# Total decay on ScalarE, a shared power for the norm, centring from PSUM, and a new written-out head order

## The chip, the cores and the metric

The kernel runs on one NeuronCore of a Trainium2 chip. The metric is the device time of one execution in microseconds. The kernel before takes 791.49 us (median of three runs, 790.57 to 791.54).

## What is computed

Inputs are float32 except the weights, which arrive as float64 words. Batch 4, 8 heads, 768 positions, head width 48; model width 384.

```
attention:  f = sigmoid(f_logit)                       # per position and channel
            state = f[t] * state + k[t] (outer) v[t]   # 48 x 48 per head, t = 0..767
            y[t]  = q[t] @ state
norm + mlp: xn = (x - mean) / sqrt(var + 1e-6) * g
            x  = x + relu(xn @ w_ch1) @ w_ch2          # 384 -> 1536 -> 384
token mix:  u  = x + (relu(x^T @ w_tok1) @ w_tok2)^T   # 768 -> 256 -> 768
mlp:        out = u + relu(u @ w_ch1') @ w_ch2'
```

## The kernel before

The attention is cut into 24 units, one for each chunk of 128 positions (six) of each batch (four). A unit's name is its number n, chunk n // 4 of batch n % 4. Its steps have short names, and a name such as `5.lnc` is step `lnc` of unit 5:

- `lf`, `lq`, `lv`: loads of the forget logits, of k and q, and of v, issued by SyncE (SP).
- `clamp` (L280), `log` (two ScalarE instructions, L284 and L285), `scan` (running sum of the logarithms, VectorE, L289), `ek` and `eq` (exponentials, L294 and L298), `km` and `qm` (k and q times these, L301 and L304).
- `tot` (L308, L309): two GpSimd copies of the last column of the sum and of `eq`, into the table `gtot` that a check reads at the end, and into `dec`, the unit's total decay.
- `kp`, `kt`: k transposed by TensorE and copied out; `sc`, `st`: scores and the state's increment; `A0`, `A1`: scores times the triangle (VectorE); `stm`, `ste`, `std`: the new state (`std`, L377, multiplies it by the total decay).
- `y`, `z` (L386, L395): the output in PSUM; `yw` orders two halves; `yc0`, `yc1`, `yt` transpose it back into the PSUM tile `y` (L438).
- `lna` (L444, L447): ScalarE copies `y` to the SBUF tile `x`, summing it; `lnc` (L454): VectorE subtracts the mean and multiplies by g; `tp` (L506), `ah`, `al` (L535, L539): transposed and split into a high and a low part. `lnv` (L457) sums squares, `lnr` (L461, L462) makes the reciprocal root on GpSimd, one unit at a time.

The weights come as 64-bit words. For each of the 24 pieces, `wN.ld` loads it, `wN.a`, `.b`, `.c` (L208, L213, L218) make a float32 of it on VectorE, `.h` is the high part (ScalarE, L230) and `.l` the low part (L231). Pieces w0 to w11 belong to the first matrix, w12 to w23 to the second.

The first MLP works on steps of three units. Steps 0 and 1 are interleaved by halves of the hidden width: `m0.3` is one hidden block of step 0 (nine matmuls, L553), `m0.h3` and `m0.l3` its parts (L568, L572), `m0.o20` nine matmuls of the second matrix for unit 2 (L583), `m0.r01` the scaled addition to x (L650), `m0.d0` the store of the finished x to `x1_d` (L653). `m0.o00`, `m0.o10`, `m0.o20` need w12 to w14, `m0.o01` and its like w15 to w17. The tile `x` has nine buffers, so that `9.lna` needs the buffer that `m0.d0` gives back.

A list of names, ORDER, sets the order of all this work up to the end of step 1 on every engine, as each engine runs its instructions in the order in which they are written. A name in the set POOL goes to GpSimd and not to VectorE. `0.kp+14` puts 14 matmuls on zeros ahead of `0.kp`. Behind the list, units and steps follow by a formula (the steady part, up to some 390 us), then token mixing and the second MLP.

```
def lna: x = xp.tile(..., tag="x") ; activation(out=x, in_=t["y"], func=Copy, accum_out=t["nm"])
def lnc: nc.vector.scalar_tensor_tensor(t["xn"], xs[n], t["nm"][:, 0:1], gln, op0=ALU.add, op1=ALU.mult)
```

Of the kernel before, what the change touches and what calls it, by code (L numbers as in the profile page):

```python
# [31 lines left out]
G_MAX = 40.0  # L32
# [14 lines left out]
    3.clamp 0.km 4.clamp 1.km 1.qm 2.km 3.km 3.qm w12.l 5.clamp 4.km 4.qm w1.l w2.l w0.l 6.clamp 5.qm 5.km w4.l  # L47
    w3.l w5.l 6.qm 6.km w13.l w14.l 7.clamp w17.l w15.l 7.qm 9.clamp w18.l 8.km w6.l 8.qm w11.l w7.l 10.clamp w8.l
    9.qm 9.km 10.qm w19.l w20.l w22.l w21.l w23.l 11.km 11.qm
""".split())  # L50
ORDER = """
    0.lf 0.clamp 1.lf 2.lf 1.clamp 0.log 3.lf 3.clamp 0.scan 0.lq 1.log 0.eq 0.ek 4.lf 0.km 0.kp+14 4.clamp 0.lv
    2.clamp 1.scan 1.lq 0.qm 0.sc 3.log 2.log 0.kt 3.scan 1.ek 2.scan 0.st 0.tot w12.ld 0.A0 0.stm 2.lq 1.lv 0.y+3
# [2 lines left out]
    2.kt w1.a 1.yw w1.b 3.lv 4.ek w2.ld 3.km w0.ld w1.c 0.tp 5.lf 0.ah 1.z 1.yc0 3.qm 1.yc1 2.st w1.h 0.al 2.A0
    2.A1 3.kp 3.kt 4.lq 0.std 2.y 2.stm 4.eq w2.a w12.l 1.yt 1.lna 2.yw 2.tot w3.ld 2.ste 2.z 2.yc0 4.tot 3.sc
    w0.a w2.b 2.yc1 w0.b 1.lnc 4.lv w4.ld 3.st 0.lnv 3.A0 2.yt 3.stm 5.clamp 2.lna 3.A1 3.ste 4.km 3.y+3 3.yw
    5.log 1.tp w2.c 3.z 2.lnc 3.yc0 w0.c 3.yc1 4.qm 6.lf 5.scan w1.l 4.kp+3 2.tp 1.ah 4.kt 4.sc 2.ah w2.h 5.lv
    5.lq 3.yt w5.ld w0.h 1.al 4.st 2.al w2.l 5.ek 3.lna w3.a w17.ld 4.A0 4.A1 m0.1 w13.ld 2.lnv 4.y w4.a w0.l w3.b  # L60
    5.eq 1.lnv 6.clamp w14.ld 6.log 4.stm w3.c 3.lnc m0.2 4.yw w4.b 4.z m0.h1 m0.0 5.qm 4.ste 4.yc0 m0.h2 w4.c
    3.tp 6.lq 5.km 5.kp w4.h w5.a 5.tot 4.yc1 m0.h0 5.sc w16.ld 6.scan w5.b w4.l w3.h m0.l2 w5.c 5.kt 4.yt 1.std
    m0.l0 w5.h 4.lna 5.st 5.A1 6.eq 5.A0 5.stm w3.l w13.a m0.l1 m0.4 5.y w5.l 7.lf 6.qm 6.ek 3.ah w14.a w13.b
    w9.ld 5.ste 5.yw m0.3 m0.h4 6.km w13.c w13.h w14.b w17.a w14.c w17.b 5.z m0.5 m0.l4 5.yc0 5.yc1 w14.h w13.l
    w15.ld m0.h3 w14.l 6.kp 6.sc 6.lv w16.a 6.kt m0.h5 5.yt 7.clamp w17.c m0.l3 3.lnv w15.a w16.b w17.h 5.lna
    w16.c m0.l5 w15.b w15.c m0.o00 m0.o20 4.lnc 7.log m0.o10 6.tot 4.tp w17.l 1.lnr w15.h w16.h 6.st 5.lnc 5.tp
    w16.l w6.ld w18.ld 2.std 4.ah w15.l m0.o01 5.ah m0.o21 3.al 5.std 2.lnr w9.a 7.scan 0.lnr m0.o11 8.lv 7.eq
    5.al 7.ek 4.al m0.r01 w8.ld 6.A0 6.stm m0.r21 8.lf 8.clamp 6.y w18.a m0.r11 m1.2 5.lnv m1.0 7.tot 7.lq m1.h2
    7.km 6.yw w6.a 6.ste 6.A1 7.lv 8.log m1.l2 7.qm m1.1 9.lf 7.kp 8.scan m1.5 4.std 6.z m1.h1 m1.l1 w9.b 4.lnv
    w18.b 7.kt m1.3 m1.h0 8.eq m1.h5 w6.b m1.l0 6.yc0 w9.c w18.c 8.ek m1.h3 w18.h 7.sc 8.lq w11.ld 3.lnr 4.lnr  # L70
    9.clamp w18.l m1.l5 9.log 6.yc1 w6.c w9.h 8.tot m1.l3 m1.4 7.st m1.o10 9.scan w8.a 6.yt 7.A0 w9.l 3.std m1.h4
    w11.a m1.o20 7.y m1.l4 w6.h w11.b 9.eq 8.km w6.l 8.qm 11.lf 5.lnr m1.o11 6.lna 9.ek w7.ld w10.ld w11.c 7.A1
    7.stm 7.yw 7.ste w11.h w22.ld w7.a w7.b w7.c w8.b w11.l m1.r11 m1.o21 m1.r21 w7.h 9.tot 11.clamp 10.lv w10.a
    8.kp w10.b w10.c 8.kt 10.lf 11.log 8.sc 7.z m1.o00 6.std w7.l w10.h 7.yc0 8.st 11.scan w10.l 8.A0 m0.7 m1.o01
    w19.ld w8.c m1.r01 w22.a w21.ld 8.y 10.clamp w22.b m0.h7 m0.10 m0.6 w22.c w8.h 9.lq 8.yw 8.A1 m0.l7 7.yc1 9.lv
    8.stm 7.yt w19.a m0.h10 m0.h6 11.ek m0.l6 11.eq 6.lnc w20.ld 8.z 8.yc0 m0.l10 8.ste 10.log m1.11 w8.l m0.9
    m1.h11 9.qm 9.km 9.kp 9.sc 10.scan 9.kt m0.8 10.ek 7.lna m0.h9 8.yc1 w19.b w20.a m1.l11 w20.b 9.st w19.c 10.eq
    m0.h8 w19.h m0.11 8.yt 10.lq 11.lv 9.A0 m0.h11 10.qm m0.l8 m1.7 8.lna m0.l9 w19.l 9.stm 9.ste w22.h 10.km 9.y
    10.kp s2.ld 9.A1 m1.8 m0.l11 9.yw m1.9 w20.c m1.h7 10.kt w20.h 8.std s0.ld s1.ld w20.l 9.z 6.tp w21.a w22.l
    8.lnc w21.b m1.h9 9.yc0 m1.l7 w23.ld 10.sc 7.std 6.lnv 10.tot m1.l9 w23.a w21.c s1.a 6.ah 6.al w23.b w23.c  # L80
    9.yc1 7.lnc 6.lnr w21.h 8.tp m1.6 8.lnv m1.h6 8.ah m1.h8 w21.l m1.10 w23.h 9.std 10.st m1.l8 10.A0 w23.l
    10.stm m1.l6 7.tp 10.ste s0.a 7.lnv 9.yt m1.h10 9.lna m0.o22 m1.l10 s0.b s1.b m0.o02 m0.o12 11.lq m0.o03
    m0.o23 s1.c m0.r03 m0.r23 m1.o22 m0.o13 7.ah m0.r13 m1.o12 s0.c m1.o02 m1.o13 m1.r13 s0.h 8.al 8.lnr m1.o03
    m1.r03 10.std m1.d0 m0.d0 m1.o23 m0.d2 m1.d1 m0.d1 10.A1 7.al s3.ld 7.lnr
""".split()


# [1028 lines left out]
```

## Time and profile before

| what | value |
|---|---|
| median of three runs | 791.49 us |
| the profiled execution | 790.75 us |
| its span, first to last instruction | 788.9 us |
| TensorE (PE) busy | 768.2 us, 97% |
| VectorE (DVE) busy | 417.8 us, 53% |
| ScalarE (ACT) busy | 325.7 us, 41% |
| GpSimd (POOL) busy | 249.0 us, 32% |
| mean granted TensorE clock | 0.992 |

The shares are means over very different parts. In the first 60 us VectorE is busy nearly all the time and TensorE waits and runs small matmuls; from then on TensorE is nearly always busy. The busy time of TensorE holds matmuls on zeros too (56 before the first load lands), so it says little by itself: how many matmuls a stretch holds says more.

### The profile page before, as it was taken

How to read it: one execution, taken by the hardware profiler on the slowest of the kernel's cores; microseconds unless marked ns; L12 is line 12 of the kernel's file. 1: busy time of each engine (PE TensorE's matmuls, PEld its weight loads, DVE VectorE, ACT ScalarE, POOL GpSimd, SP SyncE). 2: the span in 40 equal slices, each digit the busy share in tenths (PEclk: the TensorE clock that was granted, in tenths of full speed). 3: DMA queues.
4: the chain of work that ended last, by engine and by line, in shares of the span. 5: the costliest groups of instructions: out<-in, count | busy, mean ns of one | idle time of the engine just before them, and what ended most of it. 6: DMA issues, size and time to landing. Idle time of an engine off the chain costs nothing.

```text
span 788.9 us, 16758 instructions
## 1 busy us (share of the span) xinstructions
PE 768.2 (97%) x6899; PEld 717.1 (91%) x6899; DVE 417.8 (53%) x774; ACT 325.7 (41%) x817; POOL 249.0 (32%) x288
## 2 busy tenths in 40 slices
...
GB/s 236 230 155 109 222 123 35 122 129 175 141 136 128 124 192 128 146 145 52 80 132 91 192 118 91 107 84 130 111 81 91 105 146 68 112 81 102 39 1 45
DMA packets 48613, 93.39 MB, mean 118 GB/s; under 512 B 5520, under 2 KB 26128, under 8 KB 48528
## 3 DMA queue, kind: packets, MB, share of 16 engines
...
q8 instruction: 56, 0.92, 0.5%
...
## 4 chain that ended last, share of the span: by engine, by line
PE 89%; DVE 6%; DMA 2%; ACT 2%; issue 1%; SPq 0%; DVEq 0%; ACTq 0%
PE mo L583 19%; PE mo L631 19%; PE mm L610 19%; PE mm L553 16%; PE rt L792 3%; PE ht L816 3%; PE tp L506 2%; PE yT L395 2%; PE yT L386 2%; PE sc L338 1%; PE sc L350 1%; PE y L438 1%; DMA sg<-in_w 1%; DVE cu L208 1%; DVE cu L213 1%
## 5 line engine op out<-in xcount | busy, mean ns | idle before, releaser
L553 PE MATMUL mm<-xt,w1h 128*128 128x384 f32 x576 | 152.2, 345 | 4.8 <-ACT xt L535 2.3
L869 POOL TENSOR_TENSOR cs<-cs 128x384 f32<-128x384 f32 x56 | 46.5, 831 | 227.0 <-DVE cs L866 164.9
L553 PEld LDWEIGHTS mm<-xt,w1h 128*128 128x128 f32 x576 | 102.6, 189 | 7.7 <-DVE hl L572 3.2
L583 PE MATMUL mo<-w2h,hh 128*128 128x384 f32 x288 | 100.9, 350 | 0.8 <-DVE hl L572 0.8
L621 DVE SCALAR_TENSOR_TENSOR hl<-mm,hh 128x512 fp32r<-128x512 f32 x72 | 49.7, 691 | 94.1 <-ACT hh L617 94.0
L631 PE MATMUL mo<-w2h,hh 128*128 128x384 f32 x288 | 97.5, 339 | 0.0
L553 PE MATMUL mm<-xt,w1l 128*128 128x384 f32 x288 | 97.1, 337 | 0.0
L583 PE MATMUL mo<-w2h,hl 128*128 128x384 f32 x288 | 96.6, 335 | 0.0
L631 PE MATMUL mo<-w2h,hl 128*128 128x384 f32 x288 | 96.5, 335 | 0.0
L583 PE MATMUL mo<-w2l,hh 128*128 128x384 f32 x288 | 96.4, 335 | 0.0
L631 PE MATMUL mo<-w2l,hh 128*128 128x384 f32 x288 | 96.3, 335 | 0.0
L617 ACT ACTIVATE hh<-mm 128x512 fp32r<-128x512 f32 x72 | 43.0, 597 | 123.5 <-PE mm L610 123.5
L568 ACT ACTIVATE hh<-mm 128x384 fp32r<-128x384 f32 x96 | 46.5, 487 | 81.3 <-PE mm L553 79.9
L572 DVE SCALAR_TENSOR_TENSOR hl<-mm,hh 128x384 fp32r<-128x384 f32 x96 | 52.7, 552 | 39.1 <-ACT hh L568 38.5
L610 PE MATMUL mm<-xt,w1h 128*128 128x512 f32 x216 | 67.1, 392 | 0.0
L661 DVE TENSOR_TENSOR xr<-mo,xr 128x384 f32<-128x384 f32 x48 | 26.7, 556 | 73.4 <-PE mo L631 73.4
L583 PEld LDWEIGHTS mo<-w2h,hh 128*128 128x128 f32 x288 | 54.1, 188 | 2.5 <-DVE hl L572 1.1
L553 PEld LDWEIGHTS mm<-xt,w1l 128*128 128x128 f32 x288 | 54.6, 189 | 0.0
L631 PEld LDWEIGHTS mo<-w2h,hh 128*128 128x128 f32 x288 | 54.1, 188 | 0.5
L631 PEld LDWEIGHTS mo<-w2l,hh 128*128 128x128 f32 x288 | 54.1, 188 | 0.4
L583 PEld LDWEIGHTS mo<-w2l,hh 128*128 128x128 f32 x288 | 54.2, 188 | 0.0
L631 PEld LDWEIGHTS mo<-w2h,hl 128*128 128x128 f32 x288 | 54.1, 188 | 0.0
...
## 6 DMA issues: line engine op xcount, KB each, us to landing
...
```

The costliest lines, as they stand in the source:

```text
L553: nc.tensor.matmul(ps, w[:, f, k, :], x[:, k, :], start=(i == 0), stop=(i == 8))
L568: nc.scalar.activation(out=hid(f)[0], in_=t[f], func=AF.Relu)
L572: nc.vector.scalar_tensor_tensor(hl, t[f], 0.0, hh.bitcast(F32), op0=ALU.max, op1=ALU.subtract)
L583: nc.tensor.matmul(ps, x, w[:, f, :], start=(f == lo and i == 0), stop=(f == hi and i == 2))
L610: nc.tensor.matmul(ps, w[:, f, k, :], x[:, k, :], start=(i == 0), stop=(i == 8))
L617: nc.scalar.activation(out=hid(f)[0], in_=t[f], func=AF.Relu)
L621: nc.vector.scalar_tensor_tensor(hl, t[f], 0.0, hh.bitcast(F32), op0=ALU.max, op1=ALU.subtract)
L631: nc.tensor.matmul(ps, x, w[:, f, :], start=(f == lo and i == 0), stop=(f == hi and i == 2))
L661: nc.vector.tensor_tensor(x, ps, x, op=ALU.add)
L792: nc.tensor.matmul(t["r"][j][:, :DM], w[:, s, js], t[x, s], start=(s == 0 and i == 0), stop=(s == NCH - 1 and i == 2))
L816: nc.tensor.matmul(ps[:, :DM], w[:, j, js], x[:, j], start=(i == 0), stop=(i == 5))
L869: nc.gpsimd.tensor_tensor(t["u"], t["u"], t["h"], op=ALU.subtract)
```

## The change

The total decay is no longer copied. One ScalarE instruction computes exp of the last column into the table `decs`, which is kept for all units; the state is multiplied from it, and the check at the end compares it with a lower bound. `std` goes to VectorE unless POOL names it. The power of the norm is taken once for three units. `lnc` reads the PSUM tile `y` and no longer the SBUF copy `x`; `lna` still makes that copy. ORDER and POOL are new. (One line of each table is shown.)

```diff
-G_MAX = 40.0
+DEC_MIN = 4.248354255291589e-18
 POOL = set("""
-    3.clamp 0.km 4.clamp 1.km 1.qm 2.km 3.km 3.qm w12.l 5.clamp 4.km 4.qm w1.l w2.l w0.l 6.clamp 5.qm 5.km w4.l
+    0.clamp 0.km w3.l 1.km 2.qm 0.std 3.km 3.qm w2.l 4.km 4.qm w12.l w4.l w14.l w0.l w1.l 6.km w5.l 6.qm 2.std
 ORDER = """
-    0.lf 0.clamp 1.lf 2.lf 1.clamp 0.log 3.lf 3.clamp 0.scan 0.lq 1.log 0.eq 0.ek 4.lf 0.km 0.kp+14 4.clamp 0.lv
+    0.lf w12.ld 2.lf w12.a w12.b w3.ld 0.clamp 2.clamp 0.log 2.log w3.a 1.lf 4.lf w3.b 1.clamp 0.scan 4.clamp
...
-    mhalf = const.tile([128, 1], F32, name="mhalf")
-    gtot = const.tile([128, NU, NP], F32, name="gtot")
+    decs = const.tile([128, NU, NP], F32, name="decs")
+    mhalf = const.tile([128, 3], F32, name="mhalf")
...
         def pre_tot():
-            t["dec"] = sm.tile([P2, NP, 1], F32, tag="dec", name="dec")
-            nc.gpsimd.tensor_copy(gtot[:P2, n, :], t["F"][:, :, C - 1])
-            nc.gpsimd.tensor_copy(t["dec"], t["eq"][:, :, C - 1:C])
+            nc.scalar.activation(out=decs[:P2, n], in_=t["F"][:, :, C - 1], func=AF.Exp, scale=-1.0)
...
-            nc.gpsimd.tensor_tensor(s, s, t["dec"].to_broadcast([P2, NP, D]), op=ALU.mult)
+            eng("std").tensor_tensor(s, s, decs[:P2, n].rearrange("p (a o) -> p a o", o=1).to_broadcast([P2, NP, D]),
+                                     op=ALU.mult)
...
-            nc.vector.scalar_tensor_tensor(t["xn"], xs[n], t["nm"][:, 0:1], gln, op0=ALU.add, op1=ALU.mult)
+            xn, g = (a.rearrange("p (i a c) -> p i a c", i=4, a=2) for a in (t["xn"], gln))
+            y = t["y"].rearrange("p (i a c) -> p i a c", i=4, a=2)[..., :D]
+            nc.vector.scalar_tensor_tensor(xn, y, t["nm"][:, 0:1], g, op0=ALU.add, op1=ALU.mult)
...
-            nc.gpsimd.tensor_scalar(rs[:, n:n + 1], rs[:, n:n + 1], 1.0 / DM, EPS, op0=ALU.mult, op1=ALU.add)
-            nc.gpsimd.tensor_tensor(rs[:, n:n + 1], rs[:, n:n + 1], mhalf, op=ALU.pow)
+            r = rs[:, n - 2:n + 1]
+            nc.gpsimd.tensor_scalar(r, r, 1.0 / DM, EPS, op0=ALU.mult, op1=ALU.add)
+            nc.gpsimd.tensor_tensor(r, r, mhalf, op=ALU.pow)
...
-                (13, sl.e, ln_v, "lnv"), (14, sl.e, ln_r, "lnr")):
+                (13, sl.e, ln_v, "lnv"), (14, sl.e, ln_r if n % 3 == 2 else None, "lnr")):
```

The loads at the start of the program on SP, before: `first<-in_f_t` and `F<-in_f_t` are forget logits (units 0, 1, 2, then 3), k and q of unit 0 follow, then the logits of unit 4.

```order
L258 DMA first<-in_f_t 112x512 x3
L258 DMA F<-in_f_t 112x512
L266 DMA first<-in_k_t 112x512
L267 DMA first<-in_q_t 112x512
L258 DMA F<-in_f_t 112x512
L274 DMA firstv<-in_v_n 128x384
L276 DMA gln<-in_g_rep 128x384
```

The same place now; the loads from `in_w` are the weight pieces w12 and w3, of 384 KB each.

```order
L258 DMA first<-in_f_t 112x512
L199 DMA sg<-in_w 128x768
L258 DMA first<-in_f_t 112x512
L199 DMA firstv<-in_w 128x768
L258 DMA first<-in_f_t 112x512
L258 DMA F<-in_f_t 112x512
L266 DMA first<-in_k_t 112x512
L267 DMA first<-in_q_t 112x512
L258 DMA F<-in_f_t 112x512
```

Two weight pieces and one more block of logits now stand ahead of unit 0's k and q: eight loads up to q in place of six.

VectorE behind its first memsets, before, up to the first masked scores of unit 0 (`A`).

```order
L280 TENSOR_SCALAR first<-first 112x512 x2
L289 SCALAR_TENSOR_TENSOR first<-seg,first 112x512
L280 TENSOR_SCALAR first<-first 112x512
L289 SCALAR_TENSOR_TENSOR first<-seg,first 112x512
L304 TENSOR_TENSOR first<-first,eq 112x512
L289 SCALAR_TENSOR_TENSOR F<-seg,F 112x512
L289 SCALAR_TENSOR_TENSOR first<-seg,first 112x512
L357 TENSOR_TENSOR A<-sc,upper 128x256
```

The same place now, up to the q product of unit 0; `cu<-sg` and `cu<-firstv` are steps of w12 and w3.

```order
L208 TENSOR_SCALAR cu<-sg 128x384
L213 SCALAR_TENSOR_TENSOR cu<-sg,cu 128x384
L280 TENSOR_SCALAR first<-first 112x512
L208 TENSOR_SCALAR cu<-firstv 128x384
L213 SCALAR_TENSOR_TENSOR cu<-firstv,cu 128x384
L280 TENSOR_SCALAR first<-first 112x512
L289 SCALAR_TENSOR_TENSOR first<-seg,first 112x512
L280 TENSOR_SCALAR F<-F 112x512
L218 SCALAR_TENSOR_TENSOR cu<-firstv,cu 128x384
L289 SCALAR_TENSOR_TENSOR first<-seg,first 112x512
L289 SCALAR_TENSOR_TENSOR F<-seg,F 112x512
L304 TENSOR_TENSOR first<-first,eq 112x512
```

Unit 0's clamp has gone to GpSimd, and five weight steps, three clamps and two more sums stand between the start and unit 0's q product.

ScalarE at the end of ORDER, before: `x_2130<-y_2124` is `9.lna`, and `xt_98<-tp_2115` behind it is `7.ah`, which step 2 needs (units 6, 7, 8); the two rows `hh_2300` are the first of step 2.

```order
L457 ACTIVATE xn_2056,rs_89<-x_1851,nm_1852 128x384
L568 ACTIVATE hh_1711<-mm_2080 128x384
L444 ACTIVATE x_2130,nm_2131<-y_2124 128x384
L447 ACTIVATE nm_2131<-nm_2131 128x1
L535 ACTIVATE xt_98<-tp_2115 128x3x128
L568 ACTIVATE hh_2300<-mm_2286 128x384
L568 ACTIVATE hh_2300<-mm_2304 128x384
```

The same place now; `xt_98<-tp_2022` is `8.ah`, the last of the three that step 2 needs, `x_2234<-y_2061` is `9.lna`, and `hh_2257` is the first row of step 2.

```order
L537 ACTIVATE xt_98<-tp_2022 128x3x128
L429 ACTIVATE ys_2046<-yT_1990 112x2x2x64
L307 ACTIVATE decs_87<-F_1517 112x4
L458 ACTIVATE xn_1951,rs_88<-x_1916,nm_1917 128x384
L294 ACTIVATE ek_2210<-F_1764 112x512
L298 ACTIVATE eq_2232<-F_1764 112x512
L443 ACTIVATE x_2234,nm_2235<-y_2061 128x384
L446 ACTIVATE nm_2235<-nm_2235 128x1
L307 ACTIVATE decs_87<-F_1764 112x4
L570 ACTIVATE hh_2257<-mm_2243 128x384
```

`9.lna` now stands behind all three transposes that step 2 reads; before, one of them stood behind it.

## Rows read from the trace of the kernel before

**Rows 1.** The page: span, and TensorE's busy time, share and instructions.

```profile
span 788.9 us, 16758 instructions
PE 768.2 (97%) x6899; PEld 717.1 (91%) x6899; DVE 417.8 (53%) x774; ACT 325.7 (41%) x817; POOL 249.0 (32%) x288
```

**Rows 2.** By stretch: length, busy PE, PEld, DVE, ACT, POOL, PE clock, DMA share, GB/s.

```profile
0.00:10.80 10.80, 9.01 (x70) 7.95 (x70) 5.17 (x12) 6.03 (x10) 4.83 (x11) 1.00 0.83 215
...
3.80:62.80 59.00, 49.81 (x956) 42.57 (x955) 52.98 (x92) 39.55 (x96) 46.81 (x46) 0.94 0.74 212
...
63.40:123.70 60.30, 60.27 (x833) 55.59 (x834) 52.51 (x101) 33.96 (x81) 37.35 (x46) 1.00 0.47 141
```

**Rows 3.** Instructions in order of time, first 14 us: start, length, what.

```profile
3.80 0.97 DVE L280 TENSOR_SCALAR first<-first 112x512 f32<-112x512 f32 x2 [1.83 <-DMA first<-in_f_t]
...
8.86 0.69 DVE L304 TENSOR_TENSOR first<-first,eq 112x512 f32<-112x512 f32 x1 [0.60 <-DMA first<-in_q_t]
...
10.84 0.60 PE L315 MATMUL kp<-ident,first 112*128 112x112 f32 x4 [0.73 <-POOL first L301]
...
13.48 0.39 DVE L357 TENSOR_TENSOR A<-sc,upper 128x256 f32<-128x256 f32 x1
```

**Rows 4.** VectorE by line and shape, 3.8 to 62.8 us: count, busy us, mean ns.

```profile
L213 DVE SCALAR_TENSOR_TENSOR cu<-sg,cu 128x384 int32<-128x384 int32 x8 | 7.3, 913 | 0.0
L218 DVE SCALAR_TENSOR_TENSOR cu<-sg,cu 128x384 int32<-128x384 int32 x8 | 7.1, 893 | 0.1
L208 DVE TENSOR_SCALAR cu<-sg 128x384 int32<-128x384 int32 x8 | 5.8, 726 | 0.2 <-DMA sg<-in_w 0.2
...
L454 DVE SCALAR_TENSOR_TENSOR first<-x,nm,gln 128x384 f32<-128x384 f32 x3 | 3.4, 1134 | 0.0
```

**Rows 5.** VectorE, single instructions in order of time: start, length, what.

```profile
27.52 0.35 DVE L208 TENSOR_SCALAR cu<-firstv 128x384 int32<-128x384 int32 x1
...
28.33 1.01 DVE L213 SCALAR_TENSOR_TENSOR cu<-firstv,cu 128x384 int32<-128x384 int32 x2
...
62.01 0.75 DVE L218 SCALAR_TENSOR_TENSOR cu<-sg,cu 128x384 int32<-128x384 int32 x1
...
145.54 0.61 DVE L454 SCALAR_TENSOR_TENSOR xn<-x,nm,gln 128x384 f32<-128x384 f32 x1
146.06 0.61 DVE L650 SCALAR_TENSOR_TENSOR x<-mo,rs,x 128x384 f32<-128x384 f32 x1
```

**Rows 6.** GpSimd by line and shape, 3.8 to 62.8 us.

```profile
L280 POOL TENSOR_SCALAR F<-F 112x512 f32<-112x512 f32 x5 | 8.4, 1676 | 3.9 <-DMA F<-in_f_t 3.9
L231 POOL TENSOR_TENSOR w1l<-cu,w1h 128x384 fp32r<-128x384 f32 x6 | 7.5, 1260 | 3.3 <-ACT w1h L230 3.3
...
L309 POOL COPY dec<-eq 112x4 f32<-112x4 f32 x7 | 4.5, 641 | 3.0 <-ACT eq L298 3.0
```

**Rows 7.** The end of ORDER in order of time.

```profile
143.84 0.49 ACT L444 ACTIVATE x<-y 128x384 f32<-128x384 f32 x1 [19.05 <-DMA x_d<-x]
...
145.08 1.28 PE L553 MATMUL mm<-xt,w1h 128*128 128x384 f32 x2 [2.33 <-ACT xt L535]
```

**Rows 8.** The chain of waits, one piece: start, length, what.

```profile
124.01 17.20 PE mo L583 x99
```

**Rows 9.** Two stretches with a lower clock (columns as in rows 2).

```profile
20.00:30.00 10.00, 9.19 (x238) 7.44 (x238) 8.01 (x21) 6.42 (x18) 6.95 (x11) 0.70 0.92 264
...
142.50:149.30 6.80, 4.33 (x15) 3.81 (x14) 1.75 (x4) 1.65 (x5) 0.00 (x0) 0.75 0.82 275
```

**Rows 10.** What TensorE waited for from 147 to 330 us: total, times, longest.

```profile
PE mm L553 <- DVE hl L572: 2.3, 3, 0.9
```

**Rows 11.** The first of these three waits, in order of time.

```profile
165.24 1.61 POOL L304 TENSOR_TENSOR T<-T,eq 112x512 f32<-112x512 f32 x1
...
165.62 1.64 DVE L454 SCALAR_TENSOR_TENSOR xn<-x,nm,gln 128x384 f32<-128x384 f32 x1
...
167.78 0.61 PE L553 MATMUL mm<-xt,w1h 128*128 128x384 f32 x2 [0.85 <-DVE hl L572]
```

More of the change, by code (lines that the diff above doesn't have):

```diff
@@ L46 @@
 POOL = set("""
[L47 to L49 removed]
+    0.clamp 0.km w3.l 1.km 2.qm 0.std 3.km 3.qm w2.l 4.km 4.qm w12.l w4.l w14.l w0.l w1.l 6.km w5.l 6.qm 2.std
+    w16.l w15.l 5.std 7.km w9.l 8.km w6.l 3.std w10.l 8.qm 10.clamp 7.std w19.l 9.km w7.l 9.qm w20.l 10.km 10.qm
@@ L50 @@
+    w21.l w22.l 8.std 9.std 11.km 11.qm 11.std
 """.split())
 ORDER = """
-    0.lf 0.clamp 1.lf 2.lf 1.clamp 0.log 3.lf 3.clamp 0.scan 0.lq 1.log 0.eq 0.ek 4.lf 0.km 0.kp+14 4.clamp 0.lv
-    2.clamp 1.scan 1.lq 0.qm 0.sc 3.log 2.log 0.kt 3.scan 1.ek 2.scan 0.st 0.tot w12.ld 0.A0 0.stm 2.lq 1.lv 0.y+3
-    0.A1 0.ste 4.log 1.eq w12.a 1.km 3.lq 0.yw 2.eq 1.qm 4.scan 1.kp+11 0.z 2.ek 0.yc0 0.yc1 1.kt 2.qm w1.ld 1.sc
-    0.yt 2.lv w12.b 1.tot 3.eq w12.c 1.st 1.stm 2.km 1.A0 2.kp 3.tot 1.ste 3.ek 1.A1 0.lna 1.y w12.h 0.lnc 2.sc
@@ L56 @@
[L56 to L84, printed above, removed]
+    0.lf w12.ld 2.lf w12.a w12.b w3.ld 0.clamp 2.clamp 0.log 2.log w3.a 1.lf 4.lf w3.b 1.clamp 0.scan 4.clamp
```

38 lines of the change are left out of this document (35 added, 3 removed).

## The prediction

> **What bounds the kernel now.** I read the page first, then the busy time by stretch, then the waits of TensorE, and last the first 63 us and the end of ORDER in order of time. The page says that TensorE is busy 97% of a span of 788.9 us [rows 1]. The work of TensorE is the same after the change, but for matmuls on zeros, so the time can only come from places where TensorE waits or runs at half clock. There are three. From 3.8 to 62.8 us VectorE is busy 52.98 of 59 us and TensorE is fed by it [rows 2]. From 63.4 to 123.7 us TensorE loses nothing [rows 2]. At the end of ORDER it stands 2.33 us and goes on at a lower clock [rows 7, 9]. In the steady part behind, it waits three times for VectorE, 2.3 us in all [rows 10]. The reader is to see that the prize is small: beyond the head there are some 6.5 us to be had.
>
> **The head, up to 63 us.** The point at which I compare is the end of `w15.c`, with which the last of the first six pieces of the second matrix stands ready: 62.01 + 0.75 = 62.76 us before [rows 5]. By ORDER, VectorE has run 91 of its named steps by then, and 103 in the new list.
>
> *The start.* Unit 0's q landed at 8.86 us, when VectorE took it up [rows 3], and by SP's order six loads of 224 KB had been issued up to it, 1344 KB; now it is six of 224 KB and two of 384 KB, 2112 KB. The 768 KB more take 3.6 us at the 215 GB/s of this stretch [rows 2]. So unit 0's first masked scores come 3.6 us later, at some 17.1 us for 13.48 [rows 3]. ScalarE's order lies beside that: `0.ek` now stands behind the logarithm of unit 4.
>
> *Work that VectorE gains.* Up to `w15.c` it has twelve steps more: five clamps at 0.49 us (two took 0.97 [rows 3]; 2.4 us), three products at 0.69 [rows 3] (2.1), one `lnc` at 0.61 [rows 5], and one `al`, one low part and one `std` for which I take the 0.55 of a weight step (two took 1.01 us, the second starting 0.46 behind the first, so 0.09 of each is overlap [rows 5]) (1.7). Sum 6.8, less 12 x 0.09, makes 5.7 us. Seven of these steps stand ahead of the first masked scores, in time that was spent on waiting for loads: six weight steps (three of the first kind at 0.35 [rows 5], three at 0.55) and a clamp, 3.2 - 0.6 = 2.6 us. So 3.1 us are left to be paid behind it.
>
> *Work that GpSimd loses, and its lock.* A step of VectorE whose inputs both lie in SBUF takes far longer when GpSimd is at work: `lnc` took 1.64 us beside a GpSimd product that had started 0.38 us earlier [rows 11], and 0.61 us with GpSimd idle [rows 5]. In the head the excess is 8 x (0.913 - 0.55) and 8 x (0.893 - 0.55) for the second and third weight step, 8 x (0.726 - 0.35) for the first, 3 x (1.134 - 0.61) for `lnc` [rows 4], 10.2 us; with the same forms on the other tiles (four of each weight step, two `lnc`) I take 13 us. GpSimd was busy 46.8 us meanwhile [rows 2]: 0.28 us lost for each of its us. It had five clamps of 1.68 us, low parts of 1.26, and copies of the decay that took 0.64 [rows 6]. By ORDER it now has 20 steps up to `w15.c`: one clamp, nine products, eight low parts, two `std`. At 1.3 us, between the low part and the clamp, that is 26 us, and 26 x 0.28 = 7.3 us lost: 5.7 us less.
>
> Head: 3.6 + 3.1 - 5.7 = **+1.0 us**. It is the worst known term. Lower bound -3: VectorE still stood idle 6.0 of 59 us [rows 2], and with weights at hand from the start half of that may close. Upper bound +6.7, where no lock time comes back.
>
> The Trainium skill (SBUF — State Buffer, "Who interferes with whom") says that of a VectorE instruction with two SBUF inputs and a GpSimd instruction that reads SBUF the later one is fully blocked, and that one with a single SBUF input is not. The `lnc` rows agree, 1.64 for 0.61; by it `lnc` from PSUM is out of the lock altogether, which the steady part below uses from the rows alone, and the products moved to VectorE are not.
>
> **The single edits.** The total decay by ScalarE: two GpSimd copies go (counted above); ScalarE gets 24 instructions of four columns, dearer than none and cheaper than its 0.49 us copy of 384 columns [rows 7]; six in the head are 0 to 2.9 us beside its 19.4 idle ones [rows 2]: nothing. What stands behind them in its queue is the copy of k, which waits for TensorE anyway. If this cover is gone, it is those 2.9 us, inside the upper bound. The power for three units takes 16 pairs off GpSimd, which nobody waits for; off the path, nothing. Centring from PSUM: a step of this form that reads PSUM took 0.61, the one from SBUF 0.61 [rows 5]: no change when alone. But the PSUM tile `y` is now given back by VectorE instead of ScalarE; what it costs is in the new waits. Fillers: 27 matmuls on zeros instead of 34, in time that TensorE waits: nothing.
>
> **The end of ORDER: -4.2 us.** `9.lna` held ScalarE for 19.05 us, until a store of a finished x gave a buffer back; `7.ah` stood behind it, and TensorE's first matmul of step 2 waited for that [rows 7]. From 142.5 to 149.3 us TensorE started 15 matmuls [rows 9], worth 15 x 0.174 = 2.6 us (99 took 17.20 [rows 8]): 4.2 of 6.8 us lost, partly by the clock of 0.75. Now all three transposes stand ahead of `9.lna`, and the store of unit 0 comes first among its like on SP. What is late next is the last matmul group of step 1 itself. Bounds -4.2 to -2.0 (half of it, if a transpose is late for another reason).
>
> **The steady part: -1.8 us.** In the first of the three waits `lnc` was blocked: it took 1.64 us in place of 0.61, 1.03 us late, and TensorE waited 0.85 us for the step behind it [rows 11]. From PSUM it isn't blocked, and GpSimd has no copies and two of three powers less. I take 1.8 of 2.3 us [rows 10], since the steps of the weights beside it are still blocked. Bounds -2.3 to 0.
>
> **New waits from 63 to 142 us: +1.6 us.** Before, TensorE was busy 60.27 of 60.30 us [rows 2], which can't be bettered; a new order can only lose here. The nearest rows are waits of 0.85 us for VectorE [rows 11]; I take two of them. Bounds 0 to 4.
>
> **Sum.** +1.0 - 4.2 - 1.8 + 1.6 = -3.4 us. The profiled execution took 790.75 us, its span and 1.85 us around it. That makes 787.35; the median of the runs is 0.74 above the profiled one, so **788.1 us** is predicted for a median.
>
> **Rivals.**
> - *The head gains* (14%). The idle 6.0 us of VectorE [rows 2] shrink by half because it has weights to convert while loads are under way: head -3 in place of +1: 784.1 us. For it: six weight steps stand there now. Against: most of its idle time was spent on waits for TensorE's scores, which come later than before.
> - *The clock takes it back* (17%). The head's clock fell to half for 6 of the 10 us from 20 to 30 [rows 9], after a stretch with few matmuls, which lost 3 us. Unit 0's first transpose, at 10.84 us before behind a wait of 0.73 [rows 3], comes 3.6 us later, and eleven more matmuls on zeros (25 for 14) cover 1.1 of that at 0.10 us each (0.174 x 224/384): a hole of some 3 us. One more such fall, as far as TensorE and not VectorE is then late, costs 3 us: 791.1 us, no change. The Trainium skill (TensorE: Matmul & The Clock Gate, Part 1) has the half rate as the state after idling; the two rows of this trace agree, 0.70 and 0.75 behind stretches with little work.
> - *Slower: VectorE gets nothing back* (23%). Where the lock costs by the blocked VectorE instruction rather than by GpSimd's time, the 13 us stay, and the head is at +6.7 us; then `w15.l`, which stands behind `w16.l` on GpSimd with the second matmul groups right behind it on TensorE, adds 1.3 (its 1.26 [rows 6]). +8.0 - 4.2 - 1.8 + 1.6 = +3.6: 795.1 us. It decides from a head of +6.0 on. For it: GpSimd alternates with VectorE's weight steps, which are as many as before. Against: 46.8 us become some 26.
> - *The forecast* (46%), by itself 785 to 790.
>
> **Numbers.** A measurement of this kernel can tell about 0.2%, 1.6 us, from no change: faster is below 789.9, slower above 793.1. Faster: all of the first rival, 0.14, most of the forecast's 0.46 (0.40), and 0.02 of the clock: 0.56. Slower: 0.21 of the third, 0.02 of the clock: 0.23. The rest, 0.21, is the same. The range leaves out a tenth on either side: 783 to 795.
>
> **What would show it.** Right: ScalarE's wait of 19.05 us on a store is gone and step 2 follows step 1 on TensorE without a fall of the clock; `lnc` shows 0.6 us everywhere; GpSimd is busy under 30 us up to the end of `w15.c`, at 62 to 66 us; the first masked scores come near 17 us. Wrong: TensorE waits for more than 4 us between 63 and 142 us, in particular for a PSUM tile that `lnc` holds; `w15.c` ends past 68 us; or a new wait stands where `9.lna` stood.

## The result, and the profile after

The changed kernel takes **784.1 us** (median of five runs, 783.68 to 786.5), the kernel before 791.49 (five runs in all, 790.57 to 792.0): ratio 0.9915, 95% interval 0.9898 to 0.9932, so 5.4 to 8.1 us faster. Predicted were 788.1 us, with a range of 783 to 795, and 785 to 790 for the forecast itself: the result lies outside the second and 1.1 us inside the first. The profiled execution took 783.78 us; that is 6.97 us less than the profiled one of before.

The page, answering to [rows 1]: TensorE does the same work in a shorter span, but for seven matmuls on zeros (6892 for 6899).

```profile
span 782.0 us, 16682 instructions
PE 767.5 (98%) x6892; PEld 719.0 (92%) x6892; DVE 407.5 (52%) x788; ACT 328.9 (42%) x841; POOL 201.7 (26%) x194
```

Busy time by stretch, columns as in [rows 2, 9].

```profile
3.80:62.80 59.00, 51.45 (x980) 45.82 (x979) 51.91 (x105) 40.07 (x101) 29.81 (x21) 0.83 0.69 212
20.00:30.00 10.00, 9.92 (x225) 8.72 (x224) 6.49 (x15) 6.32 (x16) 5.70 (x4) 0.50 0.62 203
63.40:123.70 60.30, 59.98 (x746) 55.41 (x744) 49.11 (x99) 33.37 (x82) 23.83 (x24) 1.00 0.43 133
142.50:149.30 6.80, 6.80 (x42) 6.77 (x42) 3.22 (x7) 1.91 (x4) 0.00 (x0) 1.00 0.91 285
```

GpSimd's busy time in the head fell from 46.8 to 29.8 us. At the end of ORDER TensorE starts 42 matmuls in the stretch that held 15 before, at full clock (1.00, that is 2.4 GHz). New is the third number from the right of the second row, the clock: 0.50, so TensorE runs ten whole microseconds at half clock (1.2 GHz).

What TensorE waited for from 63.4 to 142 us (total, times, longest); from 145 to 330 us the same view has no row at all, where before three waits stood [rows 10].

```profile
PE mm L555 <- DVE hl L574: 0.3, 1, 0.3
```

VectorE by line and shape, 3.8 to 62.8 us, answering to [rows 4]: the weight steps take less, and `lnc` takes what it takes when free. The last three rows are steps that are blocked now; of the same forms the q product took 676 ns and the scan 1212 before, and a clamp takes 0.4 us when free.

```profile
L213 DVE SCALAR_TENSOR_TENSOR cu<-sg,cu 128x384 int32<-128x384 int32 x8 | 5.0, 633 | 0.1
L208 DVE TENSOR_SCALAR cu<-sg 128x384 int32<-128x384 int32 x8 | 4.4, 546 | 2.8 <-DMA sg<-in_w 2.8
L218 DVE SCALAR_TENSOR_TENSOR cu<-sg,cu 128x384 int32<-128x384 int32 x8 | 4.3, 542 | 0.0
L455 DVE SCALAR_TENSOR_TENSOR first<-y,nm,gln 128x384 f32<-128x384 f32 x3 | 1.8, 611 | 1.3 <-ACT nm L446 1.3
...
L289 DVE TENSOR_TENSOR_SCAN first<-seg,first 112x512 f32<-112x512 f32 x3 | 4.4, 1483 | 0.0
L280 DVE TENSOR_SCALAR F<-F 112x512 f32<-112x512 f32 x6 | 3.7, 609 | 0.0
L304 DVE TENSOR_TENSOR first<-first,eq 112x512 f32<-112x512 f32 x2 | 2.4, 1216 | 0.0
```

In order of time (start, length, what), answering to [rows 3, 5, 7, 11]:

```profile
12.15 1.85 POOL L301 TENSOR_TENSOR first<-first,ek 112x512 f32<-112x512 f32 x1 [7.04 <-ACT ek L294]
12.86 1.75 DVE L304 TENSOR_TENSOR first<-first,eq 112x512 f32<-112x512 f32 x1
...
14.06 0.60 PE L313 MATMUL kp<-ident,first 112*128 112x112 f32 x4 [3.44 <-POOL first L301]
14.54 2.02 DVE L289 TENSOR_TENSOR_SCAN first<-seg,first 112x512 f32<-112x512 f32 x1
...
15.44 2.18 POOL L301 TENSOR_TENSOR first<-first,ek 112x512 f32<-112x512 f32 x1
16.48 1.42 DVE L280 TENSOR_SCALAR F<-F 112x512 f32<-112x512 f32 x1
18.08 0.41 DVE L355 TENSOR_TENSOR A<-sc,upper 128x256 f32<-128x256 f32 x1
...
61.60 0.54 DVE L218 SCALAR_TENSOR_TENSOR cu<-sg,cu 128x384 int32<-128x384 int32 x1
...
142.84 0.33 PE L585 MATMUL mo<-w2h,hl 128*128 128x384 f32 x1
143.01 0.51 PE L555 MATMUL mm<-xt,w1h 128*128 128x384 f32 x2
...
161.76 0.61 DVE L455 SCALAR_TENSOR_TENSOR xn<-y,nm,gln 128x384 f32<-128x384 f32 x1
```

Unit 0's k product on GpSimd waited 7.04 us for `0.ek`, which now stands behind the logarithms of units 2, 1 and 4 on ScalarE, and TensorE waited 3.44 us for that product. Unit 0's q product took 1.75 us beside it, and the first masked scores came at 18.08 us, 4.6 us late; yet `w15.c` ends at 62.14 us, 0.6 us early. Step 2 follows step 1 without a gap at 143.01 us. `lnc` from PSUM takes 0.61 us.

Where the time went is seen by setting the same matmul of both traces side by side:

| matmul on TensorE | before | after | difference |
|---|---|---|---|
| first of the second matrix | 57.30 | 57.48 | +0.18 |
| first hidden one of step 1 | 70.27 | 70.54 | +0.27 |
| first of step 1's second half of the hidden width | 94.07 | 94.56 | +0.49 |
| first hidden one of step 2 | 145.08 | 143.01 | -2.07 |
| 55th hidden one of step 2 | 160.06 | 156.02 | -4.04 |
| first hidden one of step 3 | 196.79 | 191.89 | -4.90 |
| of step 4 | 246.50 | 240.53 | -5.97 |
| of step 5 | 295.99 | 289.33 | -6.66 |
| of step 6, and all behind it | 344.82 | 337.91 | -6.91 |

So the head gave +0.3, the stretch up to 94 us +0.2, the end of ORDER -4.5 (from there to the 55th matmul of step 2) and the steady part -2.9 us.

### The profile page after: what moved, and what is told of

The parts are those of the page before. It is cut to its first block, busy times and chain, and to the rows that moved or that the text cites. A ratio compares the mean times of both kernels' runs of the same rounds, so it can differ in the third digit from the quotient of the medians.

```text
span 782.0 us, 16682 instructions
## 1 busy us (share of the span) xinstructions
PE 767.5 (98%) x6892; PEld 719.0 (92%) x6892; DVE 407.5 (52%) x788; ACT 328.9 (42%) x841; POOL 201.7 (26%) x194
## 4 chain that ended last, share of the span: by engine, by line
PE 95%; DVE 3%; issue 1%; DMA 1%; ACT 0%; SPq 0%; ACTq 0%
PE mo L585 20%; PE mo L633 19%; PE mm L555 19%; PE mm L612 19%; PE rt L794 3%; PE ht L818 3%; PE tp L508 2%; PE yT L394 2%; PE yT L385 2%; PE sc L336 1%; PE sc L348 1%; PE y L437 1%; PE kp L313 1%; DMA firstv<-in_w 1%; DVE cu L208 1%
## 5 line engine op out<-in xcount | busy, mean ns | idle before, releaser
L555 PE MATMUL mm<-xt,w1h 128*128 128x384 f32 x576 | 150.6, 342 | 0.3 <-DVE hl L574 0.3
```

The source lines that it names most:

```text
L555: nc.tensor.matmul(ps, w[:, f, k, :], x[:, k, :], start=(i == 0), stop=(i == 8))
```

## The experiments

Ratios are to runs of the kernel before on the same chip, whose median stands in the last column.

| kernel | median us | ratio, 95% interval | before there |
|---|---|---|---|
| before, `9.lna` last | 787.58 | 0.9940, 0.9924 to 0.9956 | 791.95 |
| before, `lnc` from PSUM in the steady part | 789.72 | 0.9969, 0.9956 to 0.9981 | 791.95 |
| before, decay on ScalarE | 790.42 | 0.9981, 0.9967 to 0.9994 | 791.95 |
| before, power for three units | 789.92 | 0.9988, 0.9978 to 0.9997 | 790.91 |
| before, the first three together | 784.31 | 0.9899, 0.9882 to 0.9915 | 791.95 |
| after, `lnc` from SBUF | 785.16 | 0.9933, 0.9914 to 0.9952 | 791.45 |
| after, clamps on GpSimd | 785.50 | 0.9923, 0.9905 to 0.9941 | 791.45 |
| after, loads of weights later | 783.87 | 0.9906, 0.9890 to 0.9922 | 791.45 |
| after, all of the old start | 785.35 | 0.9930, 0.9913 to 0.9946 | 790.91 |
| the same, more zeros | 786.77 | 0.9945, 0.9928 to 0.9961 | 790.91 |
| after, more zeros | 781.98 | 0.9876, 0.9857 to 0.9896 | 791.45 |
| after, still more zeros | 784.16 | 0.9914, 0.9898 to 0.9931 | 791.25 |

**One name moved.**

```diff
-    10.stm 7.tp 10.ste s0.a 7.lnv 9.yt m1.h10 9.lna m0.o22 m1.l10 s0.b s1.b m0.o02 m0.o12 11.lq m0.o03
+    10.stm 7.tp 10.ste s0.a 7.lnv 9.yt m1.h10 m0.o22 m1.l10 s0.b s1.b m0.o02 m0.o12 11.lq m0.o03
...
-    m1.r03 10.std m1.d0 m0.d0 m1.o23 m0.d2 m1.d1 m0.d1 10.A1 7.al s3.ld 7.lnr
+    m1.r03 10.std m1.d0 m0.d0 m1.o23 m0.d2 m1.d1 m0.d1 10.A1 7.al s3.ld 7.lnr 9.lna
```

> The kernel before with one name moved: 9.lna goes to the end of ORDER. Theory (the wait of 19.05 us on ScalarE cost what the two traces show at this place): step 2 begins without TensorE's wait of 2.33 us and without the half clock behind it, and the time falls by 4.0 to 4.6 us, to some 787.2. Rival (another wait is late next: the transpose of unit 7 waits for something else, or the store behind m1.d0 on SP): 0 to -2 us, 789.5 to 791.5, and a wait of TensorE for ScalarE or a lower clock remains near 145 us.

Measured -4.4 us. The stretch at the end of ORDER looks as in the changed kernel, and the steady part's waits stay whole:

```profile
142.50:149.30 6.80, 6.80 (x42) 6.67 (x41) 4.22 (x9) 2.21 (x7) 0.00 (x0) 1.00 0.73 250
```

The theory holds: the gain of this place hangs on one name's place in ScalarE's queue. In the trace, the way from 94 us to the middle of step 2 is 3.8 us shorter than before; in traces of kernels that leave this place alone it differs by up to 0.9 us from that. Its head, which is that of before word for word, ended `w15.c` at 63.36 us for 62.76, and came to step 1 0.6 us later: less than about 1 us in the head is not told from one trace.

**`lnc` from PSUM, for units 12 to 23 alone.**

```diff
+            if n < 12:
+                nc.vector.scalar_tensor_tensor(t["xn"], xs[n], t["nm"][:, 0:1], gln, op0=ALU.add, op1=ALU.mult)
+                return
+            xn, g = (a.rearrange("p (i a c) -> p i a c", i=4, a=2) for a in (t["xn"], gln))
+            y = t["y"].rearrange("p (i a c) -> p i a c", i=4, a=2)[..., :D]
+            nc.vector.scalar_tensor_tensor(xn, y, t["nm"][:, 0:1], g, op0=ALU.add, op1=ALU.mult)
```

> The kernel before with lnc read from PSUM for units 12 to 23 alone, the steady part. Theory (lnc is held up by GpSimd when it reads SBUF): TensorE's waits for the low part of h (2.3 us in 3 waits, 0.9 the longest) go with lnc's 1.64 us, and the time falls by 2.3 to 2.9 us, to some 788.9. Rival 1 (the GpSimd copies of the decay or the powers held up the steps behind lnc as much): -0.9 us, since only the first wait goes, 790.6. Rival 2 (the PSUM tile y is given back later by VectorE): a new wait of TensorE for DVE L454, 791.5 or more.

Measured -2.2 us. TensorE's waits behind 145 us, but for the one at the end of ORDER:

```profile
PE mm L558 <- DVE hl L577: 0.9, 1, 0.9
```

1.4 of 2.3 us are gone, and there is no wait for the PSUM tile, so neither rival holds; the theory's 2.3 to 2.9 us is missed by a little. The wait that is left is the first of the three, and it stands behind an `lnc` that this run did not change: that one belongs to a unit below 12 and still reads `x`. The `lnc` at the last of the three places reads `y` now.

```profile
165.97 1.64 DVE L455 SCALAR_TENSOR_TENSOR xn<-x,nm,gln 128x384 f32<-128x384 f32 x1
...
264.09 0.60 DVE L459 SCALAR_TENSOR_TENSOR xn<-y,nm,gln 128x384 f32<-128x384 f32 x1
```

**Decay on ScalarE, std left on GpSimd.**

```diff
-            t["dec"] = sm.tile([P2, NP, 1], F32, tag="dec", name="dec")
-            nc.gpsimd.tensor_copy(gtot[:P2, n, :], t["F"][:, :, C - 1])
-            nc.gpsimd.tensor_copy(t["dec"], t["eq"][:, :, C - 1:C])
+            nc.scalar.activation(out=decs[:P2, n], in_=t["F"][:, :, C - 1], func=AF.Exp, scale=-1.0)
```

> The kernel before with the total decay by one ScalarE instruction into the kept table, in place of two GpSimd copies for each unit; std stays on GpSimd. Theory by the price of the prediction (0.28 us of VectorE for each us of GpSimd up to 63 us): 14 copies of 0.64 us less in the head are 9 us of GpSimd, and w15.c ends up to 2.5 us earlier; what of it TensorE gets back is bounded by that: 789 to 791.5. Rival 1 (a copy of four columns holds nothing up): 791.5, w15.c within 0.3 us of 62.76. Rival 2 (the 24 instructions stand in ScalarE's queue where it is late): slower than 792.

Measured -1.5 us, with nothing to be seen of it in the head: GpSimd was busy 41.5 us there for 46.8, but the weight steps took what they took before [rows 4], and `w15.c` ended at 63.60.

```profile
L213 DVE SCALAR_TENSOR_TENSOR cu<-sg,cu 128x384 int32<-128x384 int32 x8 | 7.3, 914 | 0.0
L218 DVE SCALAR_TENSOR_TENSOR cu<-sg,cu 128x384 int32<-128x384 int32 x7 | 6.4, 910 | 0.1
```

In this execution the clock stayed up behind the wait at the end of ORDER (1.00 from 142.5 to 149.3 us for 0.75), which gave this execution 1.4 us; the other eleven weren't traced, so whether the median has it isn't known. And in the steady part the three waits fell:

```profile
PE mm L551 <- DVE hl L570: 1.6, 3, 0.6
```

The time lies in the theory's range, but not for its reason: `w15.c` came no earlier.

**The power for three units alone.**

```diff
-            nc.gpsimd.tensor_scalar(rs[:, n:n + 1], rs[:, n:n + 1], 1.0 / DM, EPS, op0=ALU.mult, op1=ALU.add)
-            nc.gpsimd.tensor_tensor(rs[:, n:n + 1], rs[:, n:n + 1], mhalf, op=ALU.pow)
+            r = rs[:, n - 2:n + 1]
+            nc.gpsimd.tensor_scalar(r, r, 1.0 / DM, EPS, op0=ALU.mult, op1=ALU.add)
+            nc.gpsimd.tensor_tensor(r, r, mhalf, op=ALU.pow)
```

> The kernel before with the reciprocal root taken once for three units and nothing else. Theory of the prediction (nobody waits for these GpSimd instructions): nothing, 791.5, and TensorE still waits 2.3 us in three waits for the low part of h behind 145 us. Rival (each pair of 1.15 us stands ahead of the k and q products on GpSimd and pushes them beside a weight step and lnc of VectorE, where TensorE is late; the changed kernel with lnc from SBUF showed no such wait although lnc took 976 ns): these waits fall to under 1 us, and the time by 1.3 to 2.3 us, to 789.2 to 790.2.

Measured -1.0 us, and the three waits halved:

```profile
PE mm L553 <- DVE hl L572: 1.2, 3, 0.4
```

The rival holds in kind; both its ranges (waits under 1 us, a fall of 1.3 to 2.3) are missed by a little, and the theory's "nothing" lies just outside the interval (-0.2 to -1.7 us). At the first of these waits `lnc` is blocked as before; the weight step ahead of it is blocked less: 1.03 us, where before it took 1.48. The first row is of the kernel before.

```profile
164.22 1.48 DVE L218 SCALAR_TENSOR_TENSOR cu<-sg,cu 128x384 int32<-128x384 int32 x1
...
164.86 1.03 DVE L217 SCALAR_TENSOR_TENSOR cu<-sg,cu 128x384 int32<-128x384 int32 x1
165.43 1.61 POOL L303 TENSOR_TENSOR T<-T,eq 112x512 f32<-112x512 f32 x1
165.81 1.64 DVE L453 SCALAR_TENSOR_TENSOR xn<-x,nm,gln 128x384 f32<-128x384 f32 x1
```

**The three edits on the old head.** The edits of the first three experiments together; old order of the head, old choice of engines.

> The kernel before with the three edits together: 9.lna at the end of ORDER, lnc from PSUM for units 12 to 23, the decay by ScalarE. The old head order and the old choice of engines stay. Theory (the new head order is worth nothing: at 57 us and at 70 us the matmuls of both kernels start within 0.3 us of each other): -6.9 us or a little more, 782.5 to 785, as fast as the changed kernel. Rival (the new order is needed, as it prepares the end of ORDER or what VectorE has left at 145 us): 786.5 to 789, the changed kernel is at least 2 us faster.

Measured 784.31 us: as fast as the changed kernel. The theory holds: new order, engine choice and the shared power, which this run leaves out, together add nothing to the time that these runs can tell. The profiled execution is the slowest of the five (786.13 us). Its head is late, with `w15.c` at 63.89 us and a clock of 0.86 from 3.8 to 62.8 us; from 94 us to the middle of step 2 it is 4.4 us shorter than before, and the steady part 2.4. One wait of 0.6 us is left there, behind an `lnc` of a unit below 12.

**`lnc` from SBUF in the changed kernel.**

```diff
-            nc.vector.scalar_tensor_tensor(xn, y, t["nm"][:, 0:1], g, op0=ALU.add, op1=ALU.mult)
+            nc.vector.scalar_tensor_tensor(t["xn"], xs[n], t["nm"][:, 0:1], gln, op0=ALU.add, op1=ALU.mult)
```

> The changed kernel with lnc read from the SBUF copy x again, all else kept. Theory (in the steady part lnc is held up by GpSimd when it reads SBUF; in the head VectorE is late, and five lnc lose 0.5 us each): TensorE waits again for the low part of h behind 145 us, 1.5 to 2.5 us in all, and up to 1 us comes in the head: 785.6 to 787.6. Rival (with the copies and two of three powers gone GpSimd no longer meets lnc): no such wait, within 0.5 us of the changed kernel's 784.1.

Measured 785.16 us, 1.1 above the changed kernel with intervals that overlap. The theory fell for the steady part: TensorE has no wait there. Nor did the head lose by it in the trace: `w15.c` ended at 61.77 us. The rival's half microsecond is missed too, by less than the intervals tell apart. From 147 to 330 us `lnc` is still blocked on the mean:

```profile
L453 DVE SCALAR_TENSOR_TENSOR xn<-x,nm,gln 128x384 f32<-128x384 f32 x11 | 11.1, 1008 | 0.0
```

but where the first wait stood, GpSimd has no powers and copies ahead of its products, runs them earlier, and blocks one VectorE step in a row instead of two:

```profile
158.13 1.32 POOL L301 TENSOR_TENSOR T<-T,ek 112x512 f32<-112x512 f32 x1 [0.45 <-ACT ek L294]
...
159.42 1.28 POOL L304 TENSOR_TENSOR T<-T,eq 112x512 f32<-112x512 f32 x1
159.46 1.66 DVE L218 SCALAR_TENSOR_TENSOR cu<-sg,cu 128x384 int32<-128x384 int32 x1
161.03 0.61 DVE L453 SCALAR_TENSOR_TENSOR xn<-x,nm,gln 128x384 f32<-128x384 f32 x1
```

**Clamps of units 1 to 5 on GpSimd** (`1.clamp` to `5.clamp` added to POOL).

> The changed kernel with the clamps of units 1 to 5 back on GpSimd, in the new order. VectorE has five steps of 0.49 us less (-2.4 us), GpSimd five of 1.68 us more (8.4 us). Theory by the prediction's price (0.28 us of VectorE for each us of GpSimd): +2.4 us of blocked steps, so nothing in sum, and w15.c within 1 us of 62.1: 783.5 to 785. Rival 1 (the lock costs by the VectorE instruction that meets GpSimd, and the clamps stand mostly where VectorE waits for loads): -1 to -2.4 us. Rival 2 (the slower clamp stands in the chain from load to first scores, and lets the scores of units 1 to 4 come late): +1 to +4 us, first masked scores past 18.5 us.

Measured 785.5 us, with an interval that overlaps with the changed kernel's; in the profile `w15.c` ends 1.6 us later (63.73), and that stays to the end. The second rival is nearest: VectorE is busy 3.2 us less and still later, and unit 0's scores come at 18.98.

```profile
3.80:62.80 59.00, 51.08 (x969) 44.81 (x968) 48.74 (x96) 38.68 (x97) 36.18 (x25) 0.83 0.69 206
```

**Weight loads behind unit 0's q.**

```diff
-    0.lf w12.ld 2.lf w12.a w12.b w3.ld 0.clamp 2.clamp 0.log 2.log w3.a 1.lf 4.lf w3.b 1.clamp 0.scan 4.clamp
-    1.log 4.log 0.ek w3.c 1.scan 0.lq 0.eq 0.km 3.lf 0.lv w3.h w14.ld 0.kp+25 4.scan 1.ek w3.l 0.qm 1.eq 0.kt
+    0.lf 2.lf 1.lf 0.clamp 0.lq 0.log 2.clamp 0.scan 4.lf 1.clamp 0.ek 0.eq w12.ld 0.km w3.ld 2.log 4.clamp 1.log
+    0.kp+14 0.qm 1.scan 4.log 3.lf 0.lv w14.ld 1.ek w12.a w12.b w3.a w3.b 4.scan 1.eq w3.c w3.h w3.l 0.kt
```

> The changed kernel with another start: the loads of w12 and w3 go behind k and q of unit 0 on SP, VectorE's weight steps of them go behind unit 0's q product, unit 0's ek and eq go ahead of the logarithms of units 1, 2 and 4, and 14 matmuls on zeros instead of 25 stand ahead of the first transpose. From 0.kt on the order is kept. Theory (the late start is paid back, since VectorE's work up to w15.c is the same): the first masked scores come 3 to 4.5 us earlier, at 13.5 to 15 us, w15.c moves by less than 1 us, and the time is 783 to 785. Rival (the late start is part of the head's cost, and the new order would have gained without it): w15.c 2 to 4 us earlier, 780 to 782.

Measured 783.87 us, no difference. It does not decide: the scores came no earlier (18.37), since `0.kt` still stood behind `w3.h` on ScalarE.

```profile
PE sc L347 <- ACT kt L317: 5.5, 1, 5.5
```

**The old start in full** (`0.kt` directly behind unit 0's products, the weight steps behind its first scores; the new names alone are shown, up to `1.kp`).

```diff
+    0.lf 2.lf 1.lf 0.clamp 0.lq 0.log 2.clamp 0.scan 4.lf 1.clamp 0.ek 0.eq 0.lv 0.km w12.ld 0.kp+14 2.log 0.qm w3.ld 4.clamp
+    0.kt 1.log 0.sc 3.lf w14.ld 1.scan 0.st 4.log 2.scan 0.A0 1.ek 1.lq 1.eq w12.a 0.stm 0.tot 0.y w12.b 0.yw 0.A1 1.km w3.a
+    w3.b 4.scan 1.tot 3.clamp 3.log 2.lq 1.lv w3.c w3.h w3.l w14.a w14.b
```

> The changed kernel with the start of a4 and with the copy of unit 0's transposed k directly behind eq on ScalarE; all weight steps of the start (w12, w3, w14) stand behind unit 0's first scores on VectorE. So unit 0 starts as in the kernel before. Theory (the late start is paid back, VectorE's work up to w15.c is what counts): first masked scores at 13 to 14.5 us, and a time of 783 to 785. Rival (the late start costs what it is late, or half of it): w15.c 2 to 4 us earlier than 62.1, 780 to 782.

Now the scores come 3.4 us earlier, but `w15.c` ends 1.7 us later than in the changed kernel, at 63.79, and the kernel takes 785.35 us.

```profile
14.68 0.40 DVE L354 TENSOR_TENSOR A<-sc,upper 128x256 f32<-128x256 f32 x1
```

The rival fell; the theory is missed by a little on the slow side, with an interval that overlaps with the changed kernel's. From 3.8 to 20 us VectorE stood idle 5.0 us, for 2.3 in the changed kernel: work taken out of the wait for loads has to be done later. That the late start is the price of that cover, and a fair one, is the reading that fits; no run here sets the two apart.

**More matmuls on zeros in this start** (22, 10, 12 and 16 ahead of `0.kp`, `0.sc`, `0.y`, `1.kp`).

> The same early start, with more matmuls on zeros: 22 ahead of unit 0's first transpose, 10 ahead of its scores, 12 ahead of its output and 16 ahead of unit 1's transpose. Theory (the half clock costs the head some 2 us, as the changed kernel with more of such matmuls took 781.98, and the early start gives another 1 us or nothing): 780 to 782, with no clock below 0.8 between 10 and 40 us. Rival (the added matmuls delay the scores of units 0 and 1 by what they take, 0.1 us each at full rate): no faster than the kernel with the early start alone.

Measured 786.77 us, no faster than the early start alone, as the rival says. The theory's condition was not met either: the clock still fell, to 0.63 from 20 to 30 us. In the trace unit 0's masked scores come 0.6 us later than in that kernel (15.30 us) and `w15.c` ends 0.5 us later (64.27), so the added matmuls are in the way; the intervals of the two times overlap.

**More matmuls on zeros in the changed kernel.**

```diff
-    0.kp+25
+    0.kp+58
-    0.y
+    0.y+18
```

> The changed kernel with more matmuls on zeros: 58 for 25 ahead of unit 0's first transpose, and 18 ahead of its first output, where TensorE stood for 3.4 and 1.9 us. The granted clock, at half from 15 to 35 us in the changed kernel, should stay up for most of that. Theory (VectorE sets the pace up to 62 us, TensorE's half rate is made up for behind 35 us): the end of w15.c moves by less than 0.7 us, and the time stays within 1 us of 784.1. Rival (from 18.5 to 35.9 us TensorE ran without a gap at half rate, some 8.5 us of full-rate work, and VectorE waited for its scores 4.7 us in all): 2 to 4 us faster, 780 to 782.

Measured 781.98 us, and the interval of the ratio lies below the changed kernel's. This speaks for the rival, but the profiled execution is the slowest of the four (784.46 us; the others 780.94 to 781.99). It shows a fall of the clock from 37 to 44 us, and a stop of VectorE for which the profile shows no reason; no other trace here has one like it on VectorE in the head.

```profile
44.63 0.55 DVE L217 SCALAR_TENSOR_TENSOR cu<-firstv,cu 128x384 int32<-128x384 int32 x1 [1.77 <-issue]
```

**Still more** (also 8, 5 and 18 ahead of `1.y`, `2.y`, `4.sc`).

> The changed kernel with the more matmuls on zeros that took 781.98 (58 ahead of unit 0's first transpose, 18 ahead of its first output), and with 8, 5 and 18 of them in the holes that stood in that run's trace ahead of the outputs of units 1 and 2 and of the scores of unit 4, behind which the clock fell to half from 36 to 44 us. Theory (the half clock costs the head some 2 us in the changed kernel, and the fall from 36 to 44 us what is left of it): no clock below 0.9 up to 60 us, first hidden matmuls under 40 us, and 780 to 781.8, the fastest of all. Rival (from 36 us on VectorE sets the pace, so the clock there costs nothing): 781.5 to 782.5, the same as with the first two alone. Where the new matmuls on zeros stand in front of scores that VectorE waits for: 783 or more.

The clock now stayed at full rate all through the head. The time is 784.16 us, that of the changed kernel, so neither the theory's nor the first rival's range was met, and the first hidden matmul came at 41.31 us, not under 40:

```profile
3.80:62.80 59.00, 52.74 (x1064) 47.10 (x1063) 52.75 (x106) 40.13 (x103) 27.28 (x22) 1.00 0.73 214
20.00:30.00 10.00, 8.34 (x256) 6.84 (x255) 8.63 (x22) 8.14 (x23) 7.28 (x6) 1.00 0.85 250
```

Set beside the changed kernel, the first masked scores of unit 3 came 2.7 us earlier (34.12 us for 36.81), but `w15.c` only 0.5 us (61.64 for 62.14) and step 2 only 0.3 us (142.73). So in these two traces most of what the full clock gave was lost again before 62 us. Part of that is due to the added zeros: 18 of them ran for 1.90 us ahead of unit 4's scores, which came at 41.35 us for 40.66 with fewer zeros. Whether the half clock costs the changed kernel more than this half microsecond isn't settled. What made three runs of the kernel with fewer zeros 2 us faster stays open, and it isn't claimed as a better version.

## Why the prediction was right, point by point

**The number: right by its range, and in part by luck.** -3.4 us was forecast and -7.4 measured between the medians. The range reached down to 783 because of the rival "the head gains", which did not happen; the sign and the two gains behind the head did.

**The sign and the main cause: right.** The end of ORDER was predicted at -4.2 and measured at -4.5 in the traces and -4.4 alone (medians). What was late next was the last matmul group of step 1 itself, as said.

**The steady part: right in kind, too small, and one step wrong.** -1.8 was taken and -2.9 measured, outside the bound of -2.3 that was read from the three waits. All three waits went, and without them the same matmuls took another 0.55 us less, which no row here accounts for. The step "the power for three units takes 16 pairs off GpSimd, which nobody waits for; off the path, nothing" failed: alone it gives 1.0 us (0.2 to 1.7). Nobody waits for these instructions, but GpSimd's k and q products stand behind them, and when they run decides which VectorE steps are blocked. By the traces, the part from the middle of step 2 to step 6 changes by -2.2 (`lnc`), -1.0 (decay) and -1.1 us (power), -4.3 in sum for 2.9 together: three ways out of the same waits, each of which leaves less to the others. That is why the changed kernel with `lnc` from SBUF has no such wait either.

The Trainium skill (SBUF — State Buffer, "Who interferes with whom") adds that issue order decides who blocks. The trace agrees: in the changed kernel with `lnc` from SBUF the same `lnc` took 0.61 us when the q product began early enough to block the weight step ahead of it (1.66 us).

**The head: near in sum (+1.0 predicted, +0.3 measured), with the cause of one term and the price of another wrong.** The start came 4.6 us late and not 3.6, and not for the loads. Unit 0's q was issued at 4.07 us and landed 6.4 us later, at some 10.5 us, 1.7 us later than before; VectorE took it up at 12.86 without having waited for it, behind the weight steps, clamps and sums that now stand ahead. What held the scores was `0.ek`: VectorE ran unit 0's sum at 8.69 us for 5.58, `0.ek` then stood behind the logarithm of unit 4, and the k product that waits for it ended 3.2 us later than before. Then a scan (2.02 us) and a clamp (1.42 us), both beside steps of GpSimd, stood ahead of the masked scores on VectorE. Ahead of unit 0's k and q stand two weight pieces more, and the same four blocks of logits as before. That 3.6 was near 4.6 is luck.

The lock's term had the right size: taking each VectorE instruction by what it lasted above the usual duration of its form, some 13.9 us were lost from 3.8 to 62.8 us before and 7.6 now, 6.3 us less, where 5.7 were taken. But the price of 0.28 us for each us of GpSimd is no price. In the kernel with the decay on ScalarE alone, GpSimd was busy 5.4 us less and 14.6 us were lost; in the changed kernel with `lnc` from SBUF, 30.4 us of GpSimd went with 11.3 us lost; with the clamps on GpSimd, 36.2 us went with 6.8. Which instructions meet counts, not how long GpSimd is busy. Of the 8 us that the four groups of [rows 4] gave back (10.2 us above their free durations before, 2.2 now), 1.6 us is `lnc`, which reads PSUM; and some 3 us went to scans, clamps and q products that ran free before. The prediction also held that a step with a single SBUF input isn't blocked. A clamp has one, and the one at 16.48 us took 1.42 us beside a GpSimd product, for 0.43 free.

That the sum is near nothing is shown apart from this by the three edits on the old head. A single trace doesn't settle it to half a microsecond: in the four traces with the head as before, `w15.c` ended at 62.54 to 63.36 us. Of the marks set for the head, `w15.c` (62.14 us, 62 to 66 said) and GpSimd (29.8 us, under 30 said) were met, and the first masked scores (18.08 us, near 17 said) missed by a microsecond.

**New waits: mis-sized.** 1.6 us were taken, 0.3 us stand between 63.4 and 142 us, in one wait for VectorE.

**The rivals.** The number of "the head gains" (784.1) is the result, but not its mechanism: VectorE's idle time in the head was to shrink by half from 6.0 us and rose to 7.1, and the head gained nothing. "The clock takes it back" had its hole (3.44 us for some 3 said) and its fall, 20 us of it, and not the loss of 3 us; whether it lost less isn't settled. The lock's time did come back, so the slower rival fell at its condition.

Measured against the terms: +1.0 became +0.3, -4.2 became -4.5, -1.8 became -2.9 and +1.6 became +0.2, so -3.4 became -6.9 us between the profiled executions.
